# Two of the last weight transfers cut into unequal parts by partitions

## The chip, the core and the metric

The kernel runs on one core of one Trainium2 chip. A core has five engines with instruction streams of their own: TensorE (PE) for matrix products, VectorE (DVE), ScalarE (ACT), GpSimd (Pool) and SyncE (SP). Data come from the device memory (HBM) through sixteen DMA engines that the core's queues share; Pool and SP issue the transfers here. On-chip memory (SBUF) has 128 partitions, and a transfer names a range of partitions and what lies in each.

The metric is the time of one execution on the device in microseconds (us), lower is better. Times of several runs are told as a median. One execution was recorded by the hardware profiler: its span goes from the first to the last instruction, and its own time is a little longer.

## The reference

There are two stages. The first is a linear attention with exponential features, over 8 batches, 8 heads, 576 tokens and 64 channels:

```python
def phi(x):
    proj = np.einsum('bhsd,df->bhsf', x, w_phi)
    proj = proj - np.max(np.abs(proj), axis=-1, keepdims=True)
    return np.concatenate([np.exp(proj), np.exp(-proj)], axis=-1)
q_p, k_p = (phi(q), phi(k))
kv = np.einsum('bhsf,bhsd->bhfd', k_p, v)
z = np.sum(k_p, axis=2)
num = np.einsum('bhsf,bhfd->bhsd', q_p, kv)
den = np.einsum('bhsf,bhf->bhs', q_p, z)[..., None] + 1e-06
return (num / den)
```

Its output, with the heads side by side, is `x` of 8 x 576 x 512. The second stage mixes it in the frequency domain, with a complex 512 x 512 matrix for each of the 64 lowest frequencies (modes):

```python
X = np.fft.rfft(x, axis=1)
Xr, Xi = (np.real(X[:, :n_modes]), np.imag(X[:, :n_modes]))
Yr = np.einsum('bmd,mde->bme', Xr, w_r) - np.einsum('bmd,mde->bme', Xi, w_i)
Yi = np.einsum('bmd,mde->bme', Xr, w_i) + np.einsum('bmd,mde->bme', Xi, w_r)
Y[:, :n_modes] = Yr + 1j * Yi
y = np.fft.irfft(Y, n=S, axis=1)
u = x + y
return u + np.maximum(u @ w_ch, 0.0)
```

`w_r` and `w_i` are 64 x 512 x 512 numbers in float32 each, 67 MB, and every one of them is used once. They are by far the largest input.

## The kernel before

**Attention.** A loop over 32 steps (`S`) works through batches and pairs of heads: transposes of q and k, feature products, exponentials on ACT, maxima on DVE, then the products with v. Its result stays on chip in bfloat16 (`xs_all`), and PE multiplies it with cosines and sines at once, which gives the spectrum `XT0` and `XT1`.

**Weights.** The mode products are cut into 32 groups, `groups[k]`. The first eight hold one head each for 16 modes; groups 8 to 31 hold a block of 128 of the 512 input channels (`g` from 1 to 3) for 8 modes (`gi` from 0 to 7). Each group needs two tiles, `wr` and `wi`, of 128 partitions x 8 x 512 in bfloat16. `weights(k)` appends four entries to the list `due`: wr for y = 0 and y = 1, wi for y = 0 and y = 1. Each entry, the inner function `issue`, issues one transfer from Pool (lines 169 to 172 for groups from 8 on) into 64 of the partitions: y = 0 fills partitions 0 to 63 with the even modes, y = 1 fills 64 to 127 with the odd ones. The transfer also turns float32 into bfloat16, so a transfer that writes 512 KB reads 1 MB.

`issue_weights(n)` takes n entries from the front of `due`. During attention the strings of `plan` say how many entries are issued in each step. After it, in the loop over k up to group 30, `modes_of` (line 840) issues all entries of the group two ahead before it begins with group k (`NW = 3`). The tiles come from the pool `pw` with three buffers for each tag, so three groups fit on chip.

**Order on Pool's queue.** Pool works in the order of the program. The framework gives Pool's transfers eight completion semaphores in turn, and each transfer waits, before it is issued, for the one that used the same semaphore before: the transfer eight places earlier. A transfer into a reused buffer also waits for the matmuls that read it last. In the last third Pool has next to nothing but these transfers: four for each group, in the order wr, wr, wi, wi.

**Use.** `mode_mm` (line 438) multiplies the spectrum with a group's `wr` as soon as both halves have landed, then with `wi`. Between the two, PE does other work that is waiting (`times_w`, `flip_x`: the product of the attention output with `w_ch`). `mode_sum` adds the group into `Yacc`. After group 31 the sums are transposed, regrouped by batch (`mm_r`, `mm_z`, lines 732 and 738) and turned back into tokens (`units`, lines 778 to 801), and SP writes the output (line 929).

The lines that matter here are the issue of the weights (169), the products that wait for them (438) and the other PE work in between (694, 705, 778).

Of the kernel before, what the change touches and what calls it, by code (L numbers as in the profile page):

```python
# [26 lines left out]
def kernel(  # L27
# [11 lines left out]
    nc = tc.nc  # L39
# [68 lines left out]
    groups = [(h, -1 - G) for h in range(2) for G in range(4)]  # L108
    groups += [(g, gi) for g in range(1, 4) for gi in range(8)]

    after = [3] * 4 + [7] * 4 + [15] * 8 + [23] * 8 + [31] * 8
    W = {}

# [42 lines left out]
    def weights(k):  # L156
        g, gi = groups[k]
        W[k] = wt = {}
        for ri, w in ((0, moe_w_r), (1, moe_w_i)):
            for y in range(2):  # L160
                def issue(ri=ri, w=w, y=y):
                    if y == 0 and k == 0:
                        wt[ri] = Yacc.rearrange("p a e -> p (a e)").bitcast(BF16).rearrange(
                            "p (r m e) -> p r m e", r=2, m=8)[:, ri]
                    elif y == 0:
                        wt[ri] = pw.tile([128, 8, DMODEL], BF16, name=f"w{'ri'[ri]}", tag=f"w{ri}")
                    t = wt[ri][64 * y:64 * y + 64]
                    if gi >= 0:
                        nc.gpsimd.dma_start(  # L169
                            t.rearrange("p (m i) e -> p m (i e)", i=2),  # L170
                            w[8 * gi + y:8 * gi + 8:2, g * 128:(g + 1) * 128, :].rearrange(
                                "m (p i) e -> p m (i e)", i=2))
                    else:
                        m0 = 16 * (-1 - gi) + 8 * y
                        nc.gpsimd.dma_start(
                            t, w[m0:m0 + 8, g * 64:(g + 1) * 64, :].rearrange("m p e -> p m e"))
                due.append((k, issue))
# [384 lines left out]
    with tc.manual_schedule():  # L562
# [22 lines left out]
        for n in range(N + 2):  # L585
# [54 lines left out]
            e = n - (N + 2 - N_EARLY)  # L640
# [214 lines left out]
    with tc.manual_schedule():  # L855
        flip_x()
        flip_x()
        for k in range(k_out, 31):
            gi = groups[k][1]
# [31 lines left out]
        for m, eng in ((-2, nc.sync), (-1, nc.gpsimd), (-3, nc.sync)):  # L891
            t, gi, a, b = Yst[m]
# [7 lines left out]
        rows = slice(96, 128)  # L900
# [59 lines left out]
```

## Time and profile before

| what | value |
|---|---|
| median of 3 runs | 444.92 us (444.81 to 445.96) |
| the profiled execution, its own time | 445.59 us |
| its span | 443.8 us |
| busy share of the span: PE, DVE, ACT, Pool | 70%, 66%, 61%, 49% |
| written by DMA on chip and back | 97.86 MB, mean 221 GB/s |
| read from HBM | 163.64 MB |
| DMA share of the chain that ended last | 55% |
| of that, DMA of wi and of wr | 35% and 9% of the span |
| issue to landing of a wi transfer, median | 18.7 us |
| last wi landed, PE's last mode products begin | 405.51 us |

How to read it: the page cuts the span into 40 slices and gives the busy share of each engine in tenths, the mean busy share of the sixteen DMA engines, and the rate in GB/s of what they wrote. The chain follows the last instruction back to what released it, step by step. A window gives the same figures for any stretch in microseconds from the start of the span. A DMA row in a timeline is the instruction on Pool that issues the transfer; what stands in brackets behind it is how long the engine was idle before and what ended that. Packets of one DMA engine overlap in the records, so that a DMA engine that is never idle can have a busy share a little above 1.

### The profile page before, as it was taken

The page shows a single profiled execution, that of the slowest core. Times are in us where ns is not written, and L with a number is a line of the kernel's source. Part 1 is how long each engine was busy: PE and PEld are TensorE (multiplying, and loading weights), DVE is VectorE, ACT ScalarE, POOL GpSimd, SP SyncE. Part 2 cuts the span into 40 slices and gives each one's busy share as a digit, 9 for nine tenths or more (in the row PEclk, how much of TensorE's full clock was granted, in tenths as well). Part 3 has the DMA queues.
Part 4 walks back from the last instruction along what each step waited for, and adds up shares of the span by engine and source line. Part 5 has one row for each costly group of instructions (what it writes and reads, how often), then busy time and mean ns, then how long its engine had stood idle before and what let it go on. Part 6 is the DMA issues. An engine that isn't in the chain of part 4 may idle for free.

```text
span 443.8 us, 11840 instructions
## 1 busy us (share of the span) xinstructions
PE 310.9 (70%) x4981; PEld 201.5 (45%) x4981; DVE 293.7 (66%) x417; ACT 270.8 (61%) x567; POOL 218.1 (49%) x303
## 2 busy tenths in 40 slices
PE   0666667775767777677453767766897776789993
PEld 0455555554555655465342544433443333344441
DVE  4778879989888687878744796664232356363783
ACT  3676687886886875688633866663363254353762
POOL 6776448585566656547534554442222222200893
PEclk9999899899896596868966787888999699889997
DMA  8999999999999999999999999999999999993598
GB/s 190 243 228 218 220 228 217 229 218 218 230 221 223 221 233 221 223 233 222 223 220 222 222 222 211 211 212 211 211 211 211 211 211 211 211 207 74 183 363 328
DMA packets 60997, 97.86 MB, mean 221 GB/s; under 512 B 3936, under 2 KB 28992, under 8 KB 60944
## 3 DMA queue, kind: packets, MB, share of 16 engines
q0 software_dynamic: 51952, 76.69, 95.9%
q1 hardware_dynamic: 8832, 20.35, 13.3%
q8 instruction: 39, 0.64, 0.5%
q10 hardware_dynamic: 160, 0.07, 0.1%
q14 instruction: 14, 0.11, 0.1%
HBM read 163.64 MB, written 9.44 MB: 390 GB/s over the span
## 4 chain that ended last, share of the span: by engine, by line
DMA 55%; DVE 18%; PE 14%; issue 4%; ACT 4%; POOL 2%; ACTq 0%; SPq 0%; DVEq 0%; POOLq 0%
DMA wi<-in_moe_w_i_dram 35%; DMA wr<-in_moe_w_r_dram 9%; DMA k<-in_k_dram 8%; DVE mkq L248 7%; DVE nd L337 2%; DVE xs_all L351 2%; ACT AA L255 2%; DVE tB L330 2%; PE psB L785 2%; PE psB L778 2%; DMA kn<-in_k_dram 2%; PE psA L799 2%; PE ptr L199 1%; POOL vaug L285 1%; DMA fs<-in_w_phi_dram 1%
## 5 line engine op out<-in xcount | busy, mean ns | idle before, releaser
L285 POOL TENSOR_TENSOR vaug<-vn,ee 128x576 bf16<-128x576 f32 x64 | 72.7, 1156 | 45.7 <-ACT ee L270 43.6
L255 ACT ACTIVATE AA<-psT 128x1024 bf16<-128x1024 f32 x64 | 62.0, 1021 | 24.9 <-PE psT L223 24.2
L169 POOL DMA_DIRECT2D wr<-in_moe_w_r_dram x48 | 29.7, 620 | 78.4 <-PE psY L438 21.0
L277 ACT ACTIVATE e<-mkq 64x4 f32<-64x4 f32 (+1 forms) x128 | 26.3, 206 | 60.1 <-DVE mkq L248 57.7
L259 ACT ACTIVATE AA<-psk 128x1024 bf16<-128x1024 f32 x64 | 61.4, 1009 | 0.0
L169 POOL DMA_DIRECT2D wi<-in_moe_w_i_dram x48 | 29.9, 625 | 45.0 <-DMA wi<-in_moe_w_i_dram 13.5
L248 DVE TENSOR_REDUCE mkq<-psk 128x8 f32<-128x1024 f32 x32 | 38.7, 1211 | 0.7 <-PE psk L214 0.7
L248 DVE TENSOR_REDUCE mkq<-psq 128x8 f32<-128x1024 f32 x32 | 38.9, 1217 | 0.4 <-PE psq L214 0.3
L438 PE MATMUL psY<-wi,XT 128*32 128x512 bf16 x192 | 19.1, 477 | 26.1 <-DMA wi<-in_moe_w_i_dram 26.1
L707 ACT CAST xw<-psW 128x512 bf16<-128x512 f32 x34 | 19.8, 586 | 25.5 <-PE psW L705 25.2
L438 PEld LDWEIGHTS <-XT 128*32 128x32 bf16 x384 | 14.6, 173 | 45.8 <-issue 23.1
L705 PE MATMUL psW<-wchb,sT 128*128 128x512 bf16 x136 | 33.3, 389 | 0.0
L205 DVE COPY kT<-ptr 128x640 bf16<-128x640 bf16 x32 | 15.7, 492 | 25.3 <-PE ptr L199 25.3
L330 DVE TENSOR_TENSOR tB<-psNB,e 128x650 f32<-128x650 f32 x32 | 26.6, 832 | 8.8 <-PE psNB L320 8.4
L320 PEld LDWEIGHTS <-AA 128*128 128x128 bf16 x640 | 28.8, 110 | 7.6 <-issue 7.1
L697 DVE COPY sT<-pt 128x1024 bf16<-128x1024 bf16 x17 | 11.8, 692 | 30.5 <-PE pt L694 30.5
L223 PE MATMUL psT<-qT,w 64*128 64x512 bf16 x64 | 15.4, 471 | 23.4 <-DVE mkq L248 23.3
L199 PE MATMUL ptr<-ident_b,k 128*128 128x128 bf16 x160 | 18.1, 259 | 19.6 <-DVE qT L205 17.7
L351 DVE TENSOR_TENSOR xs_all<-nd,rden 128x640 bf16<-128x640 f32 x32 | 30.4, 951 | 1.1
L301 PE MATMUL kvz<-vaug,AA 64*128 64x65 bf16 x1152 | 28.8, 208 | 2.3 <-DVE Yacc L453 1.5
L337 DVE TENSOR_TENSOR nd<-psNA,tB 128x650 f32<-128x650 f32 x32 | 26.7, 835 | 3.8 <-DVE tB L330 0.5
L301 PEld LDWEIGHTS <-AA 64*128 64x128 bf16 x1152 | 24.5, 106 | 6.9 <-issue 2.3
(142 smaller groups left out, 726.6 us busy)
## 6 DMA issues: line engine op xcount, KB each, us to landing
wr<-in_moe_w_r_dram POOLq DMA_DIRECT2D x62, 512.0 KB, 18.9
wi<-in_moe_w_i_dram POOLq DMA_DIRECT2D x62, 512.0 KB, 18.7
out_dram<-of SPq DMA_DIRECT2D x15, 512.0 KB, 4.7
vn<-in_v_dram SPq DMA_DIRECT2D x24, 288.0 KB, 6.0
q<-in_q_dram POOLq DMA_DIRECT2D x12, 288.0 KB, 17.4
k<-in_k_dram POOLq DMA_DIRECT2D x12, 288.0 KB, 17.6
vn<-in_v_dram SPq DMA_DIRECT2D x16, 144.0 KB, 7.0
Yacc<-in_moe_w_r_dram POOLq DMA_DIRECT2D x2, 512.0 KB, 8.7
```

Of the source, the lines that this page charges most:

```text
L169: nc.gpsimd.dma_start(t.rearrange("p (m i) e -> p m (i e)", i=2), w[8 * gi + y:8 * gi + 8:2, g * 128:(g + 1) * 128, :].rearrange("m (p i) ...
L248: nc.vector.tensor_reduce(out=o, in_=i, axis=AX.X, op=ALU.max, apply_absolute_value=True)
L255: nc.scalar.activation(AA[:, 0, ab, 0:1024].rearrange("f (x j p) -> f j x p", j=2, p=64), st["psT"].rearrange("f j (x p) -> f j x p", p=64 ...
L259: nc.scalar.activation(AA[:, 1, ab, 0:1024].rearrange("p (c j f) -> p j c f", c=4, j=2), st["psk"], ACT.Exp, scale=sc)
L285: nc.gpsimd.tensor_tensor(out=vaug[:, ab, :, 0:64], in0=st["v"], in1=ee[:, ab, :].unsqueeze(2).to_broadcast([128, 9, D_]), op=ALU.mult,)
L301: nc.tensor.matmul(kvz[:, hh, ab * 65:(ab + 1) * 65], lhsT=AA[r, 1, ab, 128 * j:128 * j + 128], rhs=vaug[r, ab, j, :], start=(j == 0), sto ...
L320: nc.tensor.matmul(p[:, hh, 65 * c:65 * c + 65], lhsT=AA[:, 0, ab, x:x + 128], rhs=kvzF[:, hh, ab * 65:(ab + 1) * 65], start=True, stop=True,)
L330: nc.vector.tensor_tensor(out=tB, in0=st["psNB"], in1=e2.unsqueeze(3).to_broadcast([128, 2, NCH, 65]), op=ALU.mult,)
L337: nc.vector.tensor_tensor(out=nd, in0=st["psNA"], in1=st["tB"], op=ALU.add)
L351: nc.vector.tensor_tensor(out=xo, in0=nd[:, :, :, 0:64], in1=rden.to_broadcast([128, 2, NCH, 64]), op=ALU.mult,)
L438: nc.tensor.matmul(psY[32 * j:32 * j + 32, :], lhsT=XT[:, 16 + 32 * ri:48 + 32 * ri, 32 * i + 4 * gi + j], rhs=wt[ri][:, 2 * j + i, :], st ...
L705: nc.tensor.matmul(ps, lhsT=sT[:, x, dc, :], rhs=wchb[:, dc, :], start=(dc == 0), stop=(dc == 3))
```

## The change

Where one entry of `due` issued one transfer of 64 partitions, a table `SHARES` can now name parts. It has two entries, and the key is (group, 0 for wr or 1 for wi, y): the transfer of wi, y = 0, of group 26 is issued as 15 and then 49 partitions, and that of group 28 as 28 and then 36. All other transfers are issued whole as before. The rows that are read, the bytes that are written and the place where they land are the same. Pool has two more transfers, 304 rows instead of 302 in its program; the other engines' programs keep their order. The eight semaphores go round as before, so while both parts of a cut transfer are among the last eight, these eight hold seven transfers' worth of data.

```diff
+    SHARES = {(26, 1, 0): (15, 49), (28, 1, 0): (28, 36)}
...
                     if gi >= 0:
-                        nc.gpsimd.dma_start(
-                            t.rearrange("p (m i) e -> p m (i e)", i=2),
-                            w[8 * gi + y:8 * gi + 8:2, g * 128:(g + 1) * 128, :].rearrange(
-                                "m (p i) e -> p m (i e)", i=2))
+                        dst = t.rearrange("p (m i) e -> p m (i e)", i=2)
+                        rows = w[8 * gi + y:8 * gi + 8:2, g * 128:(g + 1) * 128, :].rearrange(
+                            "m (p i) e -> p m (i e)", i=2)
+                        p0 = 0
+                        for n in SHARES.get((k, ri, y), (64,)):
+                            nc.gpsimd.dma_start(dst[p0:p0 + n], rows[p0:p0 + n])
+                            p0 += n
```

## The prediction

> **What bounds the kernel now.** I read the page first, then the chain of waits for the last third, then the windows around the moment when the weights end, then Pool's timeline. The page's slices show DMA as the one resource that is full from the second slice to the thirty-fourth, while PE, DVE and ACT sit at 2 to 7 tenths in slices 26 to 34:
>
> ```profile
> span 443.8 us, 11840 instructions
> ...
> PE   0666667775767777677453767766897776789993
> ...
> DMA  8999999999999999999999999999999999993598
> GB/s 190 243 228 218 220 228 217 229 218 218 230 221 223 221 233 221 223 233 222 223 220 222 222 222 211 211 212 211 211 211 211 211 211 211 211 207 74 183 363 328
> ```
>
> The chain of waits says the same with names. From 288 to 405.5 us it is one weight transfer behind the other, and only then PE work:
>
> ```profile
> 326.20 19.60 DMA wi<-in_moe_w_i_dram
> 346.09 19.60 DMA wi<-in_moe_w_i_dram
> 365.98 19.60 DMA wi<-in_moe_w_i_dram
> 385.86 19.60 DMA wi<-in_moe_w_i_dram
> 405.51 0.69 PE psY L438 x5
> ```
>
> Pool's timeline shows the pace. Groups of four transfers (wr, wr, wi, wi) begin at 348.85 and 358.80, 9.95 us apart, so one 512 KB transfer takes 2.487 us. A landing takes 19.6 us, so nearly eight are under way (19.6 / 2.487 = 7.9). Each issue is preceded by 1.6 to 2.15 us of idle Pool:
>
> ```profile
> 348.85 0.61 POOL L169 DMA_DIRECT2D wr<-in_moe_w_r_dram  x1 [2.15 <-DMA wr<-in_moe_w_r_dram]
> 351.07 0.61 POOL L169 DMA_DIRECT2D wr<-in_moe_w_r_dram  x1 [1.60 <-DMA wr<-in_moe_w_r_dram]
> 353.79 0.61 POOL L169 DMA_DIRECT2D wi<-in_moe_w_i_dram  x1 [2.11 <-PE psY L438]
> 356.04 0.61 POOL L169 DMA_DIRECT2D wi<-in_moe_w_i_dram  x1 [1.64 <-DMA wi<-in_moe_w_i_dram]
> 358.80 0.61 POOL L169 DMA_DIRECT2D wr<-in_moe_w_r_dram  x1 [2.14 <-PE psW L705]
> ```
>
> The windows of one microsecond at the end of the weights matter most (next to last column: mean busy share of the sixteen DMA engines; overlapped packets count twice, so "full" is 1.12, as in every 10 us window from 330 to 398):
>
> ```profile
> 398.00:399.00 1.00, 0.47 (x5) 0.28 (x5) 0.51 (x2) 0.59 (x1) 0.00 (x0) 1.00 1.01 190
> 399.00:400.00 1.00, 0.58 (x9) 0.54 (x9) 0.36 (x1) 0.00 (x0) 0.00 (x0) 1.00 0.76 141
> ...
> 401.00:402.00 1.00, 1.00 (x12) 0.40 (x10) 0.00 (x0) 0.72 (x2) 0.00 (x0) 1.00 0.56 107
> ...
> 403.00:404.00 1.00, 1.00 (x6) 0.45 (x5) 0.00 (x0) 0.59 (x1) 0.00 (x0) 1.00 0.43 82
> 404.00:405.00 1.00, 0.63 (x3) 0.10 (x1) 0.00 (x0) 0.59 (x1) 0.00 (x0) 1.00 0.28 51
> 405.00:406.00 1.00, 0.49 (x8) 0.26 (x8) 0.00 (x0) 0.00 (x0) 0.00 (x0) 1.00 0.01 2
> ```
>
> The engines don't end together. 0.76 / 1.12 x 16 = 10.9 of them still work in 399 to 400, 8.0 in 401 to 402, 6.1 in 403 to 404, 4.0 in 404 to 405. The trace's packet records carry no engine number, but each transfer leaves sixteen completion marks, and each mark comes again 2.486 us later in the next transfer; followed so to the last transfer, the sixteen end at 398.4, 398.5, 398.7, 398.9, 399.0, 399.9, 400.6, 401.0 (eight early) and 402.8, 402.8, 404.1, 404.7, 404.8, 404.8, 404.9, 405.2 (eight late). All keep one pace, also when half of them have stopped: no engine speeds up when others idle. The late ones are late because of jolts: at each 16 KB packet of the instruction queue (39 on the page) one mark falls back by about 1.1 us, and from 286 to 403 us the jolts go round the same eight late engines in turn. Their mean end is 401.8, 3.35 us before the last.
>
> **The change, part by part.** A transfer of 64 partitions gives each engine 4, as sixteen equally spaced marks show; one partition is then 2.487 / 4 = 0.62 us of one engine. The transfers touched are the first wi half of group 26 (issued at 333.91) and of group 28 (353.79). Nothing after them is dealt differently, so every engine's end moves by what it has gained or lost in these two.
>
> *Issuing.* Two more instructions of 0.61 us on Pool, 1.22 us. They lie in Pool's idle time, 1.6 to 2.15 us before every issue; cost 0. If Pool had no such wait, all of 1.22 us would be on the path. Bytes and data packets stay; 32 completion marks of 4 bytes come on top, nothing that counts.
>
> *Fewer bytes under way.* Pool waits for the mark of the transfer eight before. With a split transfer among those eight, seven full ones are under way, 17.4 us of work for the last engine. The first engine is 6.8 us ahead of the last (405.2 - 398.4), so it has 17.4 - 6.8 = 10.6 us in its queue: it doesn't run dry. Cost 0. With no lead left it would be up to one transfer, 2.5 us.
>
> *The shares.* No row of this trace has a transfer of 15, 49, 28 or 36 partitions, so this is bounded. Below: perfect balance, -3.35 us. Above: all 49 on one engine, 45 more than its 4, 28 us. Between them I work out the two ways in which whole partitions can be dealt.
> (a) In equal counts on as many engines as divide the number: 15 as 15x1, 49 as 7x7, 28 as 14x2, 36 as 12x3, each going on round the sixteen where the last one stopped. Counting round: four engines get 10 partitions instead of 8, two get 11, one gets 12, and nine neighbours get 6. Nine gain 2 x 0.62 = 1.24 us; seven lose 1.24 to 2.49.
> (b) Filled up by the rounded share: 15 as 1 on fifteen; 49 as 4 on twelve and 1 on the next; 28 as 2 on fourteen; 36 as 3 on twelve. Twelve engines get 10, the last four get 4, 3, 1 and 0.
> I take (a) with the nine relieved engines over the eight late ones. It is the dealing whose groups answer to the rows: eight late engines that are neighbours in the round of the instruction packets, against a block of nine. Where the block begins no row shows, which is why this is a choice. Then the last engine ends at 405.2 - 1.24 = 403.9, and of the early ones the latest at most at 401.0 + 2.49 = 403.5, so the late ones still end last: **-1.24 us**.
> The Trainium skill ("DMA: Bandwidth & Descriptors", section "Why a DMA increments its semaphore by 16 and not by 1") states (a) as the general rule, the largest count up to 16 that divides, with a round-robin start for transfers from GpSimd, and reports (b) for some direct copies on trn2. By its rule the sum is -1.24 or a loss, by where the round stands; by its exception it is a loss. No run here shows either yet.
>
> *What is late next.* PE is done with its other work at 404.63 and idles 0.88 us before the last wi matmuls at 405.51. This doesn't cap the gain: group 30's wi is set by the same late engines and lands 1.24 us earlier too, and PE's work between the two (9.06 us of the 9.94) moves with it. After 405.5 nothing is touched.
>
> *Sum.* The profiled execution took 445.59 us, with a span of 443.8 and 1.8 around it. It becomes 445.59 - 1.24 = 444.35. It lies 0.67 above the median of the three timed runs, 444.92; from that the forecast is **443.7 us**.
>
> **The rivals.**
> 1. *A late engine gets more (slower).* Dealing (a) with the block elsewhere: the engine that ended at 405.2 or one of the four within 0.5 us of it gets +2 to +4 partitions, and the weights end 1.2 to 2.5 us later: 446.1 to 447.4. For it: no row ties a late engine to a partition, and a block of nine covers a block of eight in only 2 of 16 positions taken at random. Against it: positions need not be random, since every transfer so far used all sixteen and left the round at its start. It decides as soon as one of those five engines lies outside the nine. If each transfer began at the first engine, seven would get +5 and nine -2 to -8; with the late eight on the wrong side that is +3.1 us, 448.0.
> 2. *Filling up, (b).* Only four are relieved and eight are late, five of them within 0.5 us; whichever four, one of the five gets +2. The end is 404.9 + 1.24 = 406.1 or 405.2 + 1.24 = 406.4, a loss of 0.9 to 1.2 us: 445.9 to 446.2, still no measurable change.
> 3. *A price per transfer.* The smallest Pool transfers on the page (zy<-st, 32 KB) take 1.7 us from issue to landing; twice that on the path is +3.4 us, 448.3. Against it: eight transfers are always under way and the share stays at 1.12 across their seams. The Trainium skill (same page, section "Rules for kernel authors") advises against splitting a transfer into partition halves and prices a Pool transfer at a fixed 2.0 us; an estimate by that page would be +4 us. The trace speaks against it here, since the marks come at exactly 2.486 us.
> 4. *Hidden anyway.* If PE's own work became the bound before the last wi, the gain would be at most 0.88 us: 444.0. The argument on group 30 speaks against it.
>
> **How the numbers follow.** Relief over the late engines 0.42; rival 1 0.30 (a quarter of it near zero, where the engine loaded is one of the two that end at 402.8); rival 2 0.14; rival 3 0.04; rival 4 0.05; an extreme dealing on few engines 0.05. About 0.3% of the time (1.3 us) is what a measurement here can tell from no change, and 1.24 us is just under it. Of the 0.42, 0.20 come out beyond it (a late engine relieved by 3 partitions gives 1.86) and 0.22 within; rivals 2 and 4, the quarter of rival 1 add 0.27 within, together 0.5 when rounded; the rest, 0.30, is slower. The range goes from 442.9 (443.7 less one more partition, and the 0.1 that the fastest run lies under the median) to 447.2, which takes in (b) and most of rival 1 and leaves about 0.15 out; the likeliest case alone has 442.9 to 444.3.
>
> **What would show it.** Issuing: six wi issues of 0.61 us on Pool where groups 26 and 28 had four, Pool still idle before most. Shares: the DMA share falls from 1.12 later than 398.4 and reaches 0 near 403.9, in a steeper step; under rivals 1 and 2 the step is flatter and ends at 406 or later. Path: the last wi matmuls begin at 404.3 instead of 405.51 and the span ends as much earlier. Rival 3 would show as a dip in the share near 355 or 375. A PE idle of nearly 0 before the last wi would show rival 4. I am wrong if the last landing moves by anything but -1.2 us, and first of all if the nine relieved engines are not the late ones.

## The result, and the profile after

| | before | after |
|---|---|---|
| median of 22 runs each, taken side by side (us) | 445.81 (444.78 to 446.52) | 446.92 (445.5 to 448.74) |
| ratio to before, with its 95% interval | 1 | 1.0027 [1.0018, 1.0037] |
| profiled execution: its own time, its span (us) | 445.59, 443.8 | 446.85, 445.1 |

The change costs 1.1 us. The forecast was 443.7 us, a gain of 1.2, so it has the wrong sign. The measured 446.92 us lies within the stated range of 442.9 to 447.2 and within the times of its first rival.

The page of the changed kernel: its span, the DMA engines' slices, the packets and the queue that carries Pool's transfers.

```profile
span 445.1 us, 11830 instructions
...
DMA  8999999999999999999999999999999999992697
...
DMA packets 61349, 97.86 MB, mean 220 GB/s; under 512 B 4288, under 2 KB 29344, under 8 KB 61296
...
q0 software_dynamic: 52304, 76.69, 95.8%
```

The engines stay full up to the same slice. The bytes are the same, but Pool's queue q0 has 352 packets more than the 51952 of before. Two more transfers account for 32 completion marks. The other 320 are read further down; they turn out to say most.

The chain of waits, changed kernel (start, length, what), still runs through the weights to the last wi products:

```profile
369.05 16.55 DMA wi<-in_moe_w_i_dram
385.89 19.59 DMA wi<-in_moe_w_i_dram
405.52 0.69 PE psY L443 x8
```

The last products begin at 405.52, and before they began at 405.51. In this one execution the weights end at the same moment; 404.3 was forecast. The 1.3 us by which this span is longer lie at the very end, where the output is written. First the kernel before, then the changed one, windows of one microsecond (last but one: DMA share):

```profile
442.00:443.00 1.00, 0.00 (x0) 0.00 (x0) 0.00 (x0) 0.00 (x0) 0.00 (x0) 0.50 0.02 8
443.00:444.00 1.00, 0.00 (x0) 0.00 (x0) 0.00 (x0) 0.00 (x0) 0.00 (x0) 0.50 0.00 0
```

```profile
442.00:443.00 1.00, 0.00 (x0) 0.00 (x0) 0.00 (x0) 0.00 (x0) 0.00 (x0) 0.50 0.06 25
443.00:444.00 1.00, 0.00 (x0) 0.00 (x0) 0.00 (x0) 0.00 (x0) 0.00 (x0) 0.50 0.03 12
```

One DMA engine finishes the last output at 443.56, the other fifteen by 442.31; before, the last was at 442.28. That is not the change's doing: from the last weight to the end of the span it takes 38.3 us in the execution before, 39.6 here, 38.2 and 38.4 in two later profiles of the same changed kernel, and anything from 38.0 to 40.0 in the profiles of the kernels below, in which nothing after the weights differs. The weights' end itself moves too: the last mark comes at 405.48, 405.05 and 405.06 in the three profiles of the changed kernel, and at 406.31 and 404.85 in two profiles of one kernel with equal parts (e1 and h_equal below), 1.5 us apart. One profile therefore cannot show an effect of 1.1 us; the medians and the patterns have to.

Pool's timeline, changed kernel (start, length; idle time before in brackets): 333.63 and 335.80 are the parts 15 and 49, 354.61 and 356.74 the parts 28 and 36.

```profile
333.63 0.60 POOL L176 DMA_DIRECT2D wi<-in_moe_w_i_dram  x1 [2.20 <-PE psY L443]
335.80 0.77 POOL L176 DMA_DIRECT2D wi<-in_moe_w_i_dram  x1 [1.56 <-DMA wi<-in_moe_w_i_dram]
...
354.61 0.60 POOL L176 DMA_DIRECT2D wi<-in_moe_w_i_dram  x1 [1.63 <-PE pt L699]
356.74 0.62 POOL L176 DMA_DIRECT2D wi<-in_moe_w_i_dram  x1 [1.52 <-DMA wi<-in_moe_w_i_dram]
```

Pool still idles 1.5 us or more before each of the four: issuing is hidden, as forecast. The windows at the end of the weights, changed kernel:

```profile
398.00:399.00 1.00, 0.35 (x5) 0.23 (x5) 0.69 (x1) 0.59 (x1) 0.00 (x0) 1.00 1.01 190
399.00:400.00 1.00, 0.48 (x9) 0.36 (x7) 0.42 (x1) 0.00 (x0) 0.00 (x0) 1.00 0.94 176
...
401.00:402.00 1.00, 0.85 (x8) 0.34 (x10) 0.02 (x1) 0.59 (x1) 0.00 (x0) 1.00 0.71 133
...
404.00:405.00 1.00, 0.89 (x5) 0.20 (x2) 0.00 (x0) 0.72 (x2) 0.00 (x0) 1.00 0.11 20
405.00:406.00 1.00, 0.48 (x8) 0.26 (x8) 0.00 (x0) 0.08 (x1) 0.00 (x0) 1.00 0.00 0
```

Divided by the 1.12 of sixteen full engines, the share of 401 to 402 went from 8.0 engines to 10.1, that of 404 to 405 from 4.0 to 1.6. So work was moved from late engines to early ones, as intended, and yet the last products begin no earlier. The sixteen completion marks of the last weight transfer say why (the trace's landing events, us, sorted):

```
before  398.68 398.84 399.04 399.25 399.35 400.17 400.88 401.34 | 403.15 403.18 404.40 405.03 405.15 405.20 405.21 405.46
after   398.03 398.24 400.51 401.11 401.30 401.97 401.98 402.53   402.54 403.44 404.14 404.24 404.37 404.42 404.86 405.48
```

Five engines ended within 0.43 us of each other before; now one ends alone, 0.62 after the next. One late engine was left out of the relief.

**Reading the 320 packets.** They are packets of 4 bytes, like completion marks. Beyond the sixteen completion marks of each extra transfer there are 256 of them in the profile of 15 + 49 alone (e2), 64 in that of 28 + 36 alone (e3), and none with equal parts (e1). The kernel before has 2720 packets of 4 bytes in q0, sixteen for each of its 170 Pool transfers: there no engine was ever left out. On the time axis they lie in bursts, some 6 ns from packet to packet: nine bursts of 28 and one of 4 for 15 + 49, two of 8 and four of 12 for 28 + 36; 9 x 28 + 4 + 2 x 8 + 4 x 12 = 320. An engine that gets no partition of a transfer gets small fill marks in its place, four for each partition that every working engine takes. So the dealing can be read off: 49 went as 7 partitions to seven engines (9 left out, 4 x 7 = 28), 15 as one to fifteen, 28 as two to fourteen, 36 as three to twelve. That is dealing (a) of the prediction. When a burst comes says which kind of engine it is, since early engines reach the first cut some 4 us ahead of late ones; starts of the bursts of 28, changed kernel:

```
344.71 344.89 | 349.20 349.24 349.74 349.76 350.17 350.77 350.77
```

Two early and seven late engines were spared the 49. The eighth late one took 7 of the 49, and the marks of the last transfer fit 1 + 7 + 0 + 3 = 11 partitions for it, in place of 8.

The marks also say which of the late engines that is. In the first whole transfer after the cut one mark stands alone at 356.45. Taking off two paces of 2.486 us and the 2.49 us of four more partitions leaves 348.99, and in the last whole transfer before the cut the late marks are 348.96, 349.00, 349.01, 349.58, 349.96, 350.26, 351.11 and 351.23. So the loaded engine was one of the three least late, some 2.2 us ahead of the last. After both cuts it has three partitions more, 1.87 us, which nearly use up this lead, and the end of the weights stays where it was; the other seven late engines end at 404.86 or earlier, 0.6 us ahead of before. The two other profiles of the changed kernel read alike.

### The profile page after: what moved, and what is told of

Read it like the earlier page. It is cut to its first block, busy times and chain, and to the rows that moved or that the text cites. A ratio compares the mean times of both kernels' runs of the same rounds, so it can differ in the third digit from the quotient of the medians.

```text
span 445.1 us, 11830 instructions
## 1 busy us (share of the span) xinstructions
PE 307.8 (69%) x4963; PEld 200.4 (45%) x4981; DVE 294.2 (66%) x417; ACT 271.1 (61%) x567; POOL 219.6 (49%) x305
## 4 chain that ended last, share of the span: by engine, by line
DMA 49%; PE 19%; DVE 15%; ACT 7%; issue 5%; POOL 2%; SPq 0%; ACTq 0%; DVEq 0%; POOLq 0%
DMA wi<-in_moe_w_i_dram 23%; DMA wr<-in_moe_w_r_dram 13%; DMA k<-in_k_dram 6%; DVE mkq L253 5%; DMA q<-in_q_dram 4%; DVE nd L342 2%; ACT AA L260 2%; PE psY L443 2%; DVE xs_all L356 2%; PE psWe L414 2%; PE psB L790 2%; PE psA L804 2%; DVE tB L335 2%; PE psB L783 2%; DMA kn<-in_k_dram 2%
## 5 line engine op out<-in xcount | busy, mean ns | idle before, releaser
L176 POOL DMA_DIRECT2D wi<-in_moe_w_i_dram x50 | 31.4, 629 | 50.8 <-DMA wr<-in_moe_w_r_dram 14.4
L443 PE MATMUL psY<-wi,XT 128*32 128x512 bf16 x192 | 18.1, 456 | 27.0 <-DMA wi<-in_moe_w_i_dram 27.0
L710 PE MATMUL psW<-wchb,sT 128*128 128x512 bf16 x128 | 34.7, 410 | 0.7 <-issue 0.3
L325 PEld LDWEIGHTS <-AA 128*128 128x128 bf16 x640 | 27.9, 108 | 9.8 <-issue 9.6
L228 PE MATMUL psT<-qT,w 64*128 64x512 bf16 x64 | 14.2, 434 | 23.7 <-DVE mkq L253 23.6
L204 PE MATMUL ptr<-ident_b,k 128*128 128x128 bf16 x160 | 17.2, 251 | 18.8 <-DVE qT L210 15.9
```

Source lines behind the costliest of these rows:

```text
L176: nc.gpsimd.dma_start(dst[p0:p0 + n], rows[p0:p0 + n])
L325: nc.tensor.matmul(p[:, hh, 65 * c:65 * c + 65], lhsT=AA[:, 0, ab, x:x + 128], rhs=kvzF[:, hh, ab * 65:(ab + 1) * 65], start=True, stop=True,)
L443: nc.tensor.matmul(psY[32 * j:32 * j + 32, :], lhsT=XT[:, 16 + 32 * ri:48 + 32 * ri, 32 * i + 4 * gi + j], rhs=wt[ri][:, 2 * j + i, :], st ...
L710: nc.tensor.matmul(ps, lhsT=sT[:, x, dc, :], rhs=wchb[:, dc, :], start=(dc == 0), stop=(dc == 3))
```

## The experiments

Every kernel below computes the full result. Except for the tiny transfers further down, the edit is in one table, line 111, which names the parts of each cut transfer in the order in which they are issued. Microseconds are the ratio's distance from 1 times the median of the kernel before in the same session (445.2 to 446.0).

**Theory**: dealing (a), and one late engine gets more (rival 1). **Against it**: a price for each extra transfer (rival 3); the second cut does the harm; cuts cost in themselves.

### Equal parts, and each cut alone

```diff
-    SHARES = {(26, 1, 0): (15, 49), (28, 1, 0): (28, 36)}
+    SHARES = {(26, 1, 0): (16, 48), (28, 1, 0): (16, 48)}   # e1_equal, later h_equal
+    SHARES = {(26, 1, 0): (15, 49)}                         # e2_first
+    SHARES = {(28, 1, 0): (28, 36)}                         # e3_second
```

Equal parts, expected:

> Both transfers are cut into 16 and 48 partitions: every engine gets 1 and 3, so the shares stay equal, and only the two extra transfers remain of the change. Theory A (the shares: one late engine was given more): no change, the weights end as before near 405.5 us of the span, ratio 1.000. Theory B (a price for each extra transfer on the path): later by the price, +1.1 us if the two extra transfers explain all of the change, ratio 1.0025. Theory C (the program with two more Pool transfers has a later end of the output, whatever the shares): the weights end as before and the last output lands about 1.3 us later, ratio 1.0025.

The first cut alone, expected:

> Only the cut 15 + 49 of group 26. Theory A: the one late engine that is loaded keeps its +2.49 us (4 partitions), which the second cut no longer corrects by -0.57; the weights end 0.5 to 0.7 us later than with both cuts, 406.0 or more, and the time is 0.3 to 0.5% above before. Theory B: one extra transfer, half of the loss, +0.5 us, ratio 1.0012. Theory C: as with both cuts if one more transfer is enough, else nothing.

The second cut alone, expected:

> Only the cut 28 + 36 of group 28. Dealt in equal counts round the sixteen, ten engines get 5 instead of 4, two get 3 and four get 2. Theory A: some of the eight late engines are among the ten, so the weights end 0.62 us later (1 partition), ratio 1.0014. Theory B: +0.5 us as with the other cut alone, ratio 1.0012, but with the weights' end rising for all engines alike. Theory C: the weights end within 0.6 us of before and the output 1.3 us later.

Measured: equal parts 1.0011 [1.0000, 1.0023], +0.5 us; first cut alone 1.0040 [1.0024, 1.0057], +1.8 us; second alone 1.0010 [0.9996, 1.0024], +0.4 us. Two more transfers with equal shares cost 0 to 1.0 us. The harm is in the first cut, and the second, which leaves that engine out of the 28, seems to give some of it back (1.8 alone, 1.1 together; the intervals, 1.1 to 2.5 and 0.8 to 1.6, overlap). In the profile of the first cut alone one engine ends at 405.84 and the next at 403.74; with equal parts no end stands apart (the last two are 0.3 us from each other in e1).

### Moving the block of relieved engines

```diff
-    SHARES = {(26, 1, 0): (15, 49), (28, 1, 0): (28, 36)}
+    SHARES = {(26, 1, 0): (14, 49, 1)}                       # e4_block
+    SHARES = {(26, 1, 0): (13, 49, 2), (28, 1, 0): (28, 36)} # g_block
+    SHARES = {(26, 1, 0): (49, 15), (28, 1, 0): (28, 36)}    # g_swap
```

14 in front of the 49, expected:

> Group 26's transfer is cut into 14 + 49 + 1, which moves the start of the seven loaded engines by one place in the round: counted from the start of the first part, places 14, 15, 0 to 4 are loaded (+3 or +4 partitions) and places 5 to 13 relieved (-3, one of them -2). Theory A with the late engines at places 5 to 12, as the marks of the changed kernel suggest: all eight are relieved, the weights end 1.2 to 1.9 us earlier, near 403.9, ratio 0.996. Theory A with the late ones at places 8 to 15: two late engines are loaded, the weights end 1.9 to 2.5 us later, ratio 1.005. Theory B: two extra transfers, +1.1 us, ratio 1.0025. Theory C: the output's end 1.3 us later on top of whatever the weights do.

13 in front, expected:

> The first cut becomes 13 + 49 + 2; the second stays 28 + 36. The parts take 13, 7, 2, 14 and 12 engines, 48 in all, so the round closes as with the changed kernel, but the part of 49 starts one place earlier and its seven engines are the neighbours before. Theory A (one late engine is loaded): that engine now gets 5 partitions instead of 11, all eight late ones get 5 or 6 instead of 8, and the marks show 49's fill marks in one early and eight late places; the weights end 1.2 us earlier than before, near 404.2, if the price below is nothing. Theory B (a price per extra transfer, 0.25 us as the equal cut's interval 1.000 to 1.0023 would allow): three extra transfers cost 0.75 us, ratio about 0.999 with theory A's gain, 1.0017 without.

Nothing in front, expected:

> The first cut in the other order, 49 + 15; the second stays 28 + 36, so the round closes as well and the number of transfers is that of the changed kernel. Theory A: the part of 49 starts one place later, two late engines are loaded, one with 11 and one with 12 partitions instead of 8, 1.9 to 2.5 us; the weights end up to 0.6 us later than with the changed kernel, and two marks stand apart at the end instead of one; ratio 1.003 to 1.005. Theory B: the same as the changed kernel, 1.0018 to 1.0027.

Measured: 1.0033 [1.0016, 1.0050], 1.0052 [1.0034, 1.0069] and 1.0040 [1.0027, 1.0053]. All three are slower, and the gain I hoped for with 13 in front turned into the largest loss of all, 2.3 us. With 14 the bursts are again two early and seven late; with 13 in front, and with none, three early and six late. The loaded engines show in the windows of the kernel with 13 in front:

```profile
405.00:406.00 1.00, 1.00 (x6) 0.46 (x5) 0.00 (x0) 0.40 (x1) 0.00 (x0) 1.00 0.14 27
406.00:407.00 1.00, 0.86 (x4) 0.20 (x2) 0.00 (x0) 0.72 (x2) 0.00 (x0) 1.00 0.14 27
407.00:408.00 1.00, 0.33 (x8) 0.26 (x8) 0.00 (x0) 0.05 (x1) 0.00 (x0) 1.00 0.02 4
```

0.14 / 1.12 x 16 = 2.0: exactly two engines work on, and their last marks come at 407.41 and 407.62, 2.8 us after the fourteenth (404.84). My picture of one compact block of late engines had fallen with this, but not yet what takes its place.

### Is the round carried on?

If the round of the engines went on from one transfer to the next, a tiny transfer on 1, 15 or 8 engines ahead of the cut should turn it. A second one after it brings the round back to its start. The edit copies a corner of a small input into a tile that nothing reads (turns 1 and 15 shown; the others are 15 and 1, 8 and 8).

```diff
+    TURN = {(25, 0, 0): 1, (29, 0, 0): 15}
...
+                        n = TURN.get((k, ri, y), 0)
+                        if n == 1:
+                            nc.gpsimd.dma_start(turned[k, ri, y][0:1, 0:17], w_phi[0:1, 0:17])
+                        elif n:
+                            nc.gpsimd.dma_start(turned[k, ri, y][0:n, :], w_phi[0:n, 0:64])
```

The changed kernel again, beside the turns, expected:

> The changed kernel itself once more, beside kernels that turn the round. Its four parts take 15, 7, 14 and 12 engines, 48 in all, three full rounds, so the round should stand at the same place in every execution. Theory A (the shares, with the round's place kept from one execution to the next): the marks show again seven late and two early engines relieved and one late engine loaded; weights end where they did, ratio 1.002 to 1.003. Theory B (price of the extra transfers): the same ratio.

Turned by 1, by 15 and by 8, expected:

> The changed kernel with the round turned on by one engine: a tiny transfer on 1 engine at group 25, and one on 15 engines at group 29 that completes the round. The relieved block of nine moves by one place. Theory A: if the one loaded late engine sat at the far end of the block (place 15), all eight late ones are now relieved, weights end 1.2 us earlier, ratio 0.997 to 0.998; if it sat at the near end (place 5), two late ones are loaded by 3 partitions, 1.9 us, ratio 1.004. Theory B: two more transfers than the changed kernel, slower than it by as much again, ratio 1.004, whatever the turn.

> The same with the round turned on by fifteen, that is back by one. Theory A: the mirror of the turn by one; the marks speak for the near end (place 5), so this one should relieve all eight late engines: weights end 1.2 us earlier than before, ratio 0.997 to 0.998. Theory B: ratio 1.004 as with the turn by one.

> The same with the round turned by eight, so that the loaded seven fall nearly all on late engines. Theory A: the worst place, some late engine gets 3 or 4 partitions more, weights end 1.9 to 2.5 us later, ratio 1.004 to 1.006, and the early engines end before 397 us. Theory B: ratio 1.004 as with the other turns, and the weights' end no later than theirs.

Measured: the changed kernel 1.0018 [1.0007, 1.0029]; turned by 1, 1.0033 [1.0021, 1.0044]; by 15, 1.0018 [1.0006, 1.0030]; by 8, 1.0019 [1.0002, 1.0037]. The bursts are the same in all four: two early and seven late engines spared. The fill marks show that the tiny transfers went to so many engines as meant (16 marks more in each: 15 + 1, 1 + 15, 8 + 8), but they did not turn anything that matters. By the map drawn below, a round turned by 1 or by 8 would show six or three late engines spared the 49. A turn by 15 would leave that count at seven; there only the second cut can tell: the two bursts of 8 of the 28 come at 367.51 and 370.99, much as in the changed kernel (366.75 and 370.91), on an early and a late engine, and a turned round would have them on two early ones. Why nothing turned is open.

The other question, whether the round goes on from one execution to the next, needs kernels whose parts don't add up to a multiple of sixteen engines: e4 (14 + 7 + 4 = 25; its part of one partition went to four engines, since it left 12 fill marks, one on each of the other twelve) and e3 (14 + 12 = 26), each profiled once more in another session.

> The cut 14 + 49 + 1 again, unchanged: 14, 7 and 4 engines, 25, so that the round ends nine places on. If the round is kept from one execution to the next, the same program gives other engines the 49 in another execution, and the number of late engines with fill marks differs from the seven of the first profile, unless it hits one of the few places with the same pattern. If each execution starts at the same place, the pattern is the same: seven late and two early.

> The cut 28 + 36 alone again, unchanged: 14 and 12 engines, 26, ten places on. As for the last one: a round kept between executions shows the four places without a share of 36 elsewhere than at four late engines; a round that starts afresh shows the same pattern as before.

Measured: the bursts have the same pattern as the first time (seven late and two early with e4; the 28 missing on one early and one late engine, the 36 on four late ones with e3). By the map below a carried round would show e4's pattern from only two of its sixteen places and e3's from one, so these repeats speak for a round that starts at the same place in every execution. One run each, 448.26 and 446.74 us, is no time to go by.

### A map of the round, and a kernel made from it

Say that in each execution the dealing begins at place 0, that each part goes on where the one before stopped, and that the eight late engines are the same ones throughout but may lie anywhere. Then each pattern says which places hold late engines:

| kernel | engines left out, by place | bursts seen |
|---|---|---|
| changed | the 15: 15; the 49: 6 to 14; the 28: 4, 5; the 36: 0 to 3 | 49: 7 late, 2 early; 28: 1 late, 1 early; 36: early |
| 28 + 36 alone (e3) | the 28: 14, 15; the 36: 10 to 13 | 1 late, 1 early; 4 late |
| 14 + 49 + 1 (e4) | the 49: 5 to 13 | 7 late, 2 early |
| 13 + 49 + 2 | the 49: 4 to 12 | 6 late, 3 early |
| 49 + 15 | the 49: 7 to 15 | 6 late, 3 early |

One set answers to all, of all ways to put eight engines on sixteen places: late engines on 5, 6, 10, 11, 12, 13, 14 and on one of 7, 8, 9. (In the changed kernel the first cut brings early and late engines closer together, so that its 28 and 36 are harder to read by time; without these two entries the same set is left.) They are spread over ten places. A block of nine neighbours can't hold all eight, wherever it begins, so by this map no cut with a 49 relieves them all. But 25 + 39 can: by the same dealing 25 goes to five engines, five partitions each, and leaves eleven out; 39 goes to thirteen, three each. As 25 + 39 and then 39 + 25, the 25s begin at 0 and at 15, where all five are early, and each late engine gets 6 partitions in place of 8. In the reverse order, 39 + 25 and 25 + 39, they hit two late engines each time. The same parts, the same number of transfers, only the order differs.

```diff
-    SHARES = {(26, 1, 0): (15, 49), (28, 1, 0): (28, 36)}
+    SHARES = {(26, 1, 0): (25, 39), (28, 1, 0): (39, 25)}   # h_spare
+    SHARES = {(26, 1, 0): (39, 25), (28, 1, 0): (25, 39)}   # h_hit
+    SHARES = {(26, 1, 0): (25, 39)}                         # h_once
```

> Parts of 25 + 39 and of 39 + 25 partitions: by the dealing that the fill marks have shown, 25 goes to five engines (5 each) and 39 to thirteen (3 each), so 4 x 20 fill marks... in all 11 x 20 + 3 x 12 for each pair, 512 more marks than with equal parts. Theory: the dealing begins at the same engine in every execution and the parts follow each other round; the patterns of the changed kernel, e3, e4, g_block and g_swap then put the eight late engines on places 5, 6, 10 to 14 and one of 7 to 9 of that round (the first dealt engine being 0). No run of nine engines next to each other holds all eight of these, so no cut with 49 could spare them all; eleven relieved engines can. Here the two parts of 25 begin at places 0 and 15, where all five engines are early ones, and every late engine gets 3 + 3 partitions in place of 4 + 4: -2 x 0.62 = -1.24 us at the end of the weights, against 0 to 1.0 us that two cuts into equal parts cost. Expected: 0.9970 to 0.9995 of the kernel before, the fill marks of 25 on eight late and three early engines, and no lone late end in the last transfer. Rival one, places that cannot be foretold (the three small transfers did not turn them): late engines are among the five loaded ones, 1.002 to 1.006, with one or more ends standing apart. Rival two, every uneven cut costs, wherever it falls: 1.002 to 1.004 here and with the order reversed alike.

> The same four parts in the other order, 39 + 25 and 25 + 39. Theory: the parts of 25 now begin at places 13 and 2; the late engines on 13 and 14 get 5 + 3, those on 5 and 6 get 3 + 5, the other four 3 + 3: four late engines keep their 8 partitions, so the end of the weights does not move, and the two extra transfers are left: 1.000 to 1.0025, that is 0.3 to 0.5% behind the first order, with the last transfer's late ends in two groups of four some 1.2 us apart. Rival one: no telling, the two orders differ either way. Rival two, every uneven cut costs: the same time as the first order.

> The first cut alone, 25 + 39. Theory: every late engine gets 3 partitions in place of 4, -0.62 us, against 0 to 0.5 us for one more transfer: 0.9985 to 1.000, and no lone late end. Rival one: a late engine among the five loaded ones gets 5 + 3 (or 5 alone) in place of 4, up to +2.5 us, 1.001 to 1.006. Rival two: half of what the two cuts cost, 1.001 to 1.002.

> Both transfers cut into 16 + 48, which leaves every engine its 8 partitions: the price of two more transfers, again, beside the cuts of 25 and 39. Theory: 1.000 to 1.002 as in e1 (1.0011), and the uneven cuts are to be read against it: the first order 0.2 to 0.4% below it, the reversed order level with it. Rival two: uneven cuts of either order are slower than this by 0.1% or more.

Measured in one session:

| kernel | ratio to before |
|---|---|
| 25 + 39, 39 + 25: no late engine loaded | 0.9990 [0.9977, 1.0003] |
| 39 + 25, 25 + 39: late engines loaded | 1.0024 [1.0010, 1.0038] |
| 25 + 39 alone | 1.0002 [0.9991, 1.0013] |
| 16 + 48 twice (equal) | 1.0004 [0.9992, 1.0016] |

The two orders lie 1.5 us apart and their intervals don't touch, as foretold. The single cut came out a little above the 0.9985 to 1.000 expected. The reversed order was also expected level with the equal parts; it lies 0.9 us behind them (the intervals just overlap), which the map does not explain. The page of the kernel that spares the late engines has the expected number of fill marks (52496 - 51952 = 544 = 32 + 512):

```profile
DMA packets 61541, 97.86 MB, mean 221 GB/s; under 512 B 4480, under 2 KB 29536, under 8 KB 61488
...
q0 software_dynamic: 52496, 76.69, 96.3%
```

The bursts of 20 marks of the first 25 begin at 344.6 to 345.1 on three engines and at 348.4 to 350.7 on eight in the first order: three early and eight late, as the map said. For the other order the map says five early and six late; the bursts begin at 348.58, 348.60, 348.66, 348.76, 349.31 and then at 350.43, 350.78, 350.93, 351.25, 351.25, 352.10: five and six. The gap is narrower there: the last early engine of that execution was only 1.1 us ahead of the first late one when the cut came (347.73 against 348.87 in the transfer before it). In the profiles of these two kernels the weights end at 404.77 and 404.68, no difference, and the two groups of late ends 1.2 us apart that were expected of the reversed order are not there; the profiled execution of the second was its fastest of twelve (444.9 against a median of 446.52). The times, not that profile, carry the verdict.

That the sparing order gains on the kernel before was still open (its interval took in 1), so it ran once more beside the changed kernel:

> The cut that spares all eight late engines (25 + 39, 39 + 25) once more, beside the changed kernel itself. If its 0.999 is a gain, it comes out at 0.998 to 0.9995 again; if two more transfers eat the whole of the 1.24 us, at 1.0000 or above. The pattern of the fill marks must be the same as before: 3 early and 8 late engines without a share of the first 25.

> The changed kernel itself (15 + 49, 28 + 36), in the same session. One late engine holds 11 partitions in place of 8: 1.0015 to 1.004 of the kernel before, and 0.2 to 0.4% behind the cut that spares the late engines. If the placement does not matter, the two come out alike.

Measured: sparing 0.9982 [0.9968, 0.9997], 445.26 us against 446.02; changed kernel 1.0018 [1.0002, 1.0033]. The two lie 1.6 us apart and their intervals don't touch. The windows and the chain of the sparing kernel:

```profile
399.00:400.00 1.00, 1.00 (x8) 0.46 (x6) 0.69 (x1) 0.00 (x0) 0.00 (x0) 1.00 0.86 162
...
401.00:402.00 1.00, 1.00 (x11) 0.36 (x8) 0.00 (x0) 0.48 (x1) 0.00 (x0) 1.00 0.79 147
...
403.00:404.00 1.00, 0.75 (x4) 0.13 (x2) 0.00 (x0) 0.66 (x2) 0.00 (x0) 1.00 0.31 57
404.00:405.00 1.00, 0.64 (x9) 0.28 (x10) 0.00 (x0) 0.00 (x0) 0.00 (x0) 1.00 0.00 0
```

```profile
384.72 19.60 DMA wi<-in_moe_w_i_dram
404.36 0.69 PE psY L443 x6
```

The last products begin at 404.36 in place of 405.51, 1.15 us earlier, and the marks' end moved from 405.46 to 404.32. From there to the end of the span it takes 38.3 us in both, so the span is as much shorter: 442.6 for 443.8. This is the picture that the prediction drew for the change, but it is one execution, the fastest of its twelve (444.38 us); in the first session's profile of the same kernel the last products begin at 404.82, 0.69 us earlier than before, and equal parts, which relieve nobody, had them at 404.89 in one profile. So the size of the gain rests on the medians, and it is small: 0.8 us the second time, with an interval that only just leaves 1 out, and 0.45 the first time, with one that does not.

The marks show a limit of this cut. The places 0 to 3 get 13 partitions in place of 8, 3.1 us more, and in both profiles the late ends are a group of twelve instead of eight (401.75 to 404.32 here): four early engines have become late ones.

### All cuts together

The last column but one is the number of partitions that the most loaded late engine has above a plain share, by the map.

| cut | excess | us against before |
|---|---|---|
| 25 + 39, 39 + 25 (two sessions) | -2 | -0.45, -0.8 |
| 25 + 39 | -1 | +0.1 |
| equal (two sessions) | 0 | +0.5, +0.2 |
| 39 + 25, 25 + 39 | 0 | +1.1 |
| 28 + 36 | +1 | +0.4 |
| 15 + 49, 28 + 36 (three sessions) | +3 | +1.2, +0.8, +0.8 |
| 14 + 49 + 1 | +3 | +1.5 |
| 15 + 49 | +4 | +1.8 |
| 49 + 15, 28 + 36 | +4 | +1.8 |
| 13 + 49 + 2, 28 + 36 | +4 | +2.3 |

A straight line through these fourteen gives 0.36 us for each partition and 0.3 us for the cuts as such (correlation 0.90). The worst fit is the reverse order, +1.1 where the line says 0.3. The three kernels with tiny transfers (+1.5, +0.8, +0.8 at an excess of +3) are not in it, since they have two transfers more.

## Why the prediction was right or wrong

*Issuing at no cost, fewer bytes under way at no cost*: right, as far as the runs can tell. Pool idles before each issue (timeline above), the DMA share stays at 1.13, 1.12 and 1.12 through the windows of 340 to 370 with the parts under way, and equal parts cost 0.5 [0, 1.0] and 0.2 [-0.4, 0.7] us. A few tenths are not excluded; the line above says 0.3.

*The dealing*: right. (a) was shown by the fill marks to the last packet; filling up, rival 2, would leave three engines out of the 49, not nine. The Trainium skill ("DMA: Bandwidth & Descriptors", section "Why a DMA increments its semaphore by 16 and not by 1") states this dealing as its general rule, with neighbouring engines from a round-robin cursor for transfers from GpSimd; the traces agree on the counts and on parts that follow one another round, and its exception for some direct copies did not occur here. The turning of that cursor by the tiny transfers, which the rule would lead one to expect, did not show.

*The nine relieved engines over the eight late ones*: this is the step that failed. "It is the dealing whose groups answer to the rows: eight late engines that are neighbours in the round of the instruction packets, against a block of nine." The order in which the instruction packets go round says nothing about the order of dealing, and by the map the late engines are no neighbours there: 5, 6, one of 7 to 9, and 10 to 14. The block lay on 6 to 14. The late engine on 5 was outside it and got 11 partitions in place of 8, 1.9 us of work more, and its mark stands alone at 405.48, where 404.2 was to come: the relief of the others reaches nobody. Measured: a loss of 0.8 to 1.2 us in three sessions. Only a part of this loss has an account. The loaded engine had been 2.2 us ahead of the last, so its 1.9 us hold the end of the weights (405.48, 405.05 and 405.06 in three profiles, 405.46 before) and don't push it out; two cuts into equal parts cost 0.2 and 0.5 us; where the rest, about half of the loss, arises no profile shows. The chance of 0.42 for the step was too high: the text itself had counted 2 favourable positions of 16 and then set that aside by a likeness of two numbers, eight and nine. By the map there was no favourable position at all.

*The size of relief*: not contradicted once the late engines are really spared, but not shown either. The sum said -1.24 us; the profiles of the sparing cut have -1.14 and -0.69 for the end of the weights, against a single profile before, and the runs -0.8 [-1.4, -0.1] and -0.45 [-1.0, 0.1], with a few tenths lost to the extra transfers. The slope over all cuts is 0.36 and not 0.62 us for each partition. That it is smaller agrees with the lead of the engine on place 5, but by this lead the first cut alone should cost some 0.3 us beside the price of the cut, and 1.8 were measured, with the weights' end 0.4 us later in its profile. So the line sums up the runs and is no account of them.

*What is late next*: right, as far as the profiles reach. PE idled 0.88 us before the last wi products in the profile before and still 0.62 us in the sparing one, where they begin 1.15 us earlier; PE's work between moved along.

*The base*: the three runs shown before (444.92) lay low; six sessions gave 445.2 to 446.0 for the same kernel. Of the 3.2 us between forecast and result 0.9 come from that, 1.2 from the relief that did not come and 1.1 from the loss that came instead, of which about half is open.

*The rivals*: rival 1 is what happened to the dealing, but that 446.92 lies in its 446.1 to 447.4 is partly luck: those times stand on a base that was 0.9 us too low, and the loss itself, 0.8 to 1.2 us, is at or below the lower end of the 1.2 to 2.5 worked out. The engine loaded was not one of the five last that the rival named but one of the least late, for which the prediction had put the loss near zero. Rival 3, +3.4 us for two extra transfers, is excluded by equal parts; the estimate of +4 us worked out from the Trainium skill (same page; the fixed 2.0 us stands in its section "Anatomy of one DMA — SWDGE (gpsimd) path") likewise disagrees with the +0.5 and +0.2 measured. Against rival 4 speaks, for the sparing cut, that PE still idled 0.62 us before the last products.

*Open*: half of the loss, and why the reversed order is slower than equal parts; where the dealing begins in absolute terms, why the tiny transfers did not turn it, and which of the places 7 to 9 is late. The map was drawn from five kernels and then foretold two patterns and the order of their times, but it was not tried on a third.

## What to carry to other kernels

When the DMA engines of a core end at different times, uneven transfers can move work between them, but only if you know which engines a part lands on: measure that first. A cut by partitions leaves a print, fill packets of 4 bytes on the engines left out, and their times say early or late. Do the relief through parts that load few engines, test both orders of the same parts, and price the cut with equal parts beside it; a small gain that hangs on a position is a coin toss until then.

## What the runs showed of the hardware

- A transfer from Pool that uses fewer than sixteen engines still makes packets on the others: 4 bytes each, as many as the pieces that each working engine gets (28 for 7 partitions of four pieces, 4 for 1, 8 for 2, 12 for 3), some 6 ns apart. Together 320 here; a burst of 28 takes its engine about 0.16 us (344.72 to 344.88).
- The pattern of engines that a part spares was the same in a second execution of programs whose cut parts use 25, 26 and 36 engines in all, and it was not moved by transfers on 1, 8 or 15 engines ahead of the parts.
- The end of the output varies by more than the effect studied: from the last weight to the end 38.0 to 40.0 us over the profiles, with the last output's final packet at 442.28 or 443.56 while fifteen engines end by 442.3 in both. The end of the weights moved by up to 1.5 us between two profiles of one kernel (404.85 and 406.31). For an effect of 0.3% the medians of several runs and the pattern within the trace were needed; spans alone would have misled.
